# A gated feed-forward layer on one core: all 28 column tiles multiplied in pairs, first products of eight pairs run ahead, and two pairs' weights sent from a second queue

## The chip, the cores and the metric

The kernel runs on one core of one Trainium2 chip. The metric is the device time of one execution in microseconds (us); lower is better. Most executions of a kernel agree within a few tenths of a per cent; the profile is of one execution, and its span (first to last instruction) is some 2 us shorter than the device time. Each ratio is quoted with its 95% interval.

## The reference, cut to what matters

```python
B, S, D, F = 32, 32, 1024, 3584          # bfloat16 inputs
def reference(x, w_gate, w_up, w_down):
    return (gelu_tanh(x @ w_gate) * (x @ w_up)) @ w_down
```

There are 1024 rows of x. The kernel works transposed: 28 tiles of 128 columns of F, each over two halves of 512 rows (call them half 0 and half 1), with 8 contraction steps of 128 (k = 0 to 7) for gate and for up.

## The kernel before: the parts that matter

Two tiles (a "left" and a "right" one), two halves of the rows and two halves of k make a 2 x 2 by 2 x 2 block product. Done directly it takes 8 block products; the kernel does it with 7, in a scheme of sums and differences. Two of the seven multiply plain bf16 weights and plain x. The other five multiply *sums* of x (array `S`, made once) by *sums* of weights (array `T`, made for each pair), which are kept as fp32r (32-bit). One product is 8 matmuls of 128x128 by 128x512 (4 for gate, 4 for up).

A small scheduler sorts each engine's instructions (TensorE excepted, which keeps program order) by an `at` value and adds the semaphores. So `at` is an order and not a time: an engine that waits for one item holds up all behind it.

```python
# The opening: four tiles on half 0, directly, as the k blocks arrive ...
steps = [(m, j, k) for k in range(DK - KO) for j in range(2) for m in range(4)]
...
    op = mm(2 * m + j, first[:, j, k, tile(m)*P:(tile(m)+1)*P], xT[0][:, k, :], ...)
    if k == 3 and m < 2:                       # product 1 of pairs 0 and 1 is kept
        act(kept[m][:, j, :], bank(2 * m + j), COPY, 10.5)
    if (m, j) == (3, 1) and k == 3:            # second half of x: four DMA transposes
        for k0 in range(0, DK, 2): load_x(1, k0, k0 + 2, [op])
# ... then two of these tiles on half 1, directly (32 matmuls) ...
load_near(10)                                  # right-hand weights of pairs 0, 1   (1 MB, SyncE)
load_pairs(1, 0, 11, slice(0, 4))              # left-hand weights of pairs 2, 3    (1 MB, SyncE)
load_pairs(1, 0, 11, slice(4, 8))
load_pairs(1, 1, 12)                           # right-hand weights of pairs 2, 3   (1 MB, SyncE)
# ... then products 1 and 2 of pairs 2 and 3 run ahead (32 matmuls), while VectorE makes the sums
for p in (2, 3):
    ...
# ... then 13 pairs: EARLY = 4 of them have 5 products left (40 fp32r matmuls),
# the other 9 have all 7 (16 bf16 and 40 fp32r matmuls), then the down projection
for p in range(NP):
    short, last = p < EARLY, p == NP - 1
    ...
```

`load_x` is a DMA that transposes on its way in. Why products 1 and 2 run ahead: they need only weights and half 0 of x, so they give TensorE work while the sums are being made.

## Time and profile before

| | before |
|---|---|
| device time, median of 6 runs | 275.26 us |
| span of the profile | 272.7 us |
| TensorE (PE) busy | 268.1 us, 98% |
| VectorE / ScalarE busy | 69% / 46% |
| opening: 128 bf16 matmuls | 4.61 to 32.42 us |
| four early pairs: 160 fp32r matmuls | 32.42 to 69.15 us |
| a late pair | 12.56 us |

The page of the profile has the busy time of each engine, then the span cut in 40 slices with the busy share in tenths (PEclk is the granted clock of TensorE in tenths), then the chain of work that ended last.

```profile
PE 268.1 (98%) x1186; PEld 188.1 (69%) x1200; DVE 189.2 (69%) x221; ACT 125.7 (46%) x195; POOL 45.4 (17%) x27
...
PE   8999999999999999999999999999999999999995
...
PEclk9999999999999999999999999999999999999999
DMA  7999412954700090047005000995011000001112
...
PE 98%; issue 0%; DVE 0%
```

TensorE is never idle, at full clock, and the chain is TensorE alone: the time is the number of matmuls times their rate. The DMA row shows the one place where something else is near its limit: the first four slices (up to about 27 us) are full. (The share adds up the times of all DMA packets and divides by 16 engines; packets can overlap.)

The timeline of PE (columns: start, length, engine, line, operation, output and inputs, shapes, count):

```profile
4.61 28.16 PE L117 MATMUL ps<-arena 128*128 128x512 bf16 x126
32.42 36.66 PE L117 MATMUL ps<-S,T 128*128 128x512 f32 x160
69.15 1.67 PE L117 MATMUL ps<-arena 128*128 128x512 bf16 x7
```

The first line is the whole opening, in one piece. The second is the four early pairs: 36.73 us from start to start for 160 matmuls. (A few records of matmuls are missing, hence 126 for 128.) And the timeline of PE's weight loads in the middle of the opening; the bracket tells how long the weight loader was idle before, and what ended that:

```profile
25.56 0.55 PEld L117 LDWEIGHTS ps<-arena 128*128 128x128 bf16 x4 [0.33 <-DMA arena<-in_w_gate_dram]
26.47 0.55 PEld L117 LDWEIGHTS ps<-arena 128*128 128x128 bf16 x4 [0.36 <-DMA arena<-in_w_up_dram]
```

These are the weights of the second pair of tiles to run ahead. They come just as TensorE wants them, with nothing to spare.

### The profile page before, as it was taken

What the parts mean: (1) busy time and instruction counts of PE and PEld (TensorE: products, weight loads), DVE (VectorE), ACT (ScalarE), POOL (GpSimd) and SP (SyncE); (2) the same over time, 40 slices, a digit from 0 to 9 for tenths busy, and PEclk for the clock granted to TensorE, in tenths of its full rate; (3) what the DMA queues carried; (4) which work ended last, traced back from release to release, by engine and by line L of the source; (5) the groups of instructions that cost most, each with busy time, mean ns of one, the idle gap of its engine ahead of it and who ended that gap; (6) DMA issues with size and microseconds to landing.
All of it is one profiled execution on the core that took longest, in us unless ns stands there. A gap on an engine that the chain in (4) does not pass through costs nothing.

```text
span 272.7 us, 3266 instructions
## 1 busy us (share of the span) xinstructions
PE 268.1 (98%) x1186; PEld 188.1 (69%) x1200; DVE 189.2 (69%) x221; ACT 125.7 (46%) x195; POOL 45.4 (17%) x27
## 2 busy tenths in 40 slices
PE   8999999999999999999999999999999999999995
PEld 4444588888767686868676776664447888888884
DVE  1059978988583939374664739289962999999942
ACT  2344757566556474646455564521220112255561
POOL 1000032035326060524335160000000000000000
PEclk9999999999999999999999999999999999999999
DMA  7999412954700090047005000995011000001112
GB/s 184 270 207 300 117 39 60 281 202 124 186 0 0 21 286 2 0 129 179 1 4 154 0 2 0 302 350 159 0 38 38 2 0 0 1 2 58 38 58 77
DMA packets 44783, 26.42 MB, mean 97 GB/s; under 512 B 8416, under 2 KB 44768, under 8 KB 44768
## 3 DMA queue, kind: packets, MB, share of 16 engines
q1 hardware_dynamic: 42544, 24.25, 32.3%
q10 hardware_dynamic: 2224, 1.97, 2.8%
q8 instruction: 9, 0.15, 0.2%
q14 instruction: 6, 0.05, 0.1%
HBM read 22.28 MB, written 2.10 MB: 89 GB/s over the span
## 4 chain that ended last, share of the span: by engine, by line
PE 98%; issue 0%; DVE 0%
PE ps L117 98%; DVE arena L117 0%
## 5 line engine op out<-in xcount | busy, mean ns | idle before, releaser
L117 PE MATMUL ps<-S,T 128*128 128x512 f32 x520 | 122.0, 393 | 0.0
L117 PEld LDWEIGHTS ps<-S,T 128*128 128x128 f32 x520 | 97.7, 188 | 21.3
L117 ACT ACTIVATE tmp<-ps 128x512 f32<-128x512 f32 x64 | 38.1, 598 | 62.0 <-PE ps L117 62.0
L117 POOL TENSOR_TENSOR T<-arena 128x1024 fp32r<-128x1024 bf16 x21 | 44.7, 2149 | 117.1 <-PE ps L117 66.7
L117 PE MATMUL ps<-arena 128*128 128x512 bf16 x261 | 59.0, 379 | 0.8
L117 PE MATMUL ps<-T,S 128*128 128x512 f32 x224 | 51.3, 390 | 0.0
L117 ACT ACTIVATE ps<-ps 128x512 f32<-128x512 f32 x52 | 30.2, 583 | 42.0 <-PE ps L117 42.0
L117 DVE TENSOR_TENSOR hT<-tmp,ps 128x512 bf16<-128x512 f32 x56 | 37.2, 684 | 17.3 <-PE ps L117 14.9
L117 DVE TENSOR_TENSOR T<-arena,T 128x1024 fp32r<-128x1024 bf16 x40 | 48.4, 1217 | 0.1
L117 PEld LDWEIGHTS ps<-arena 128*128 128x128 bf16 x272 | 25.1, 98 | 33.4 <-issue 3.4
L117 PEld LDWEIGHTS ps<-T,S 128*128 128x128 f32 x224 | 42.1, 188 | 8.8
L117 DVE TENSOR_TENSOR tmp<-ps,tmp 128x512 f32<-128x512 f32 x26 | 18.0, 692 | 41.9 <-PE ps L117 41.9
L117 DVE TENSOR_TENSOR T<-arena 128x1024 fp32r<-128x1024 bf16 x19 | 22.7, 1218 | 7.4 <-PE ps L117 7.4
L117 PE MATMUL ps<-arena,hT 128*128 128x512 bf16 x109 | 24.0, 379 | 0.2
L117 DVE TENSOR_TENSOR ps<-ps,tmp 128x512 f32<-128x512 f32 x30 | 20.9, 695 | 2.8 <-PE ps L117 2.8
L117 PEld LDWEIGHTS ps<-arena,hT 128*128 128x128 bf16 x112 | 10.9, 98 | 13.2 <-issue 0.3
L117 ACT ACTIVATE tmp<-tmp 128x512 f32<-128x512 f32 x26 | 16.4, 632 | 4.2 <-DVE tmp L117 3.5
L117 DVE TENSOR_TENSOR S<-hT 128x1024 fp32r<-128x1024 bf16 x14 | 16.6, 1218 | 0.0
L117 ACT ACTIVATE T<-arena 128x1024 fp32r<-128x1024 bf16 x13 | 13.7, 1055 | 0.0
L117 PE MATMUL ps<-S 128*128 128x512 f32 x56 | 12.9, 389 | 0.0
L117 PEld LDWEIGHTS ps<-S 128*128 128x128 f32 x56 | 10.5, 188 | 2.2
L117 ACT ACTIVATE S<-arena 128x1024 fp32r<-128x1024 bf16 x9 | 9.4, 1057 | 4.3 <-PE ps L117 3.0
(25 smaller groups left out, 62.1 us busy)
## 6 DMA issues: line engine op xcount, KB each, us to landing
arena<-in_w_down_dram SPq DMA_DIRECT2D x4, 1792.0 KB, 10.5
arena<-in_w_gate_dram SPq DMA_DIRECT2D x11, 512.0 KB, 5.5
arena<-in_w_up_dram SPq DMA_DIRECT2D x11, 512.0 KB, 6.4
out_dram<-arena SPq DMA_DIRECT2D x12, 128.0 KB, 1.7
arena<-in_w_up_dram ACTq DMA_DIRECT2D x4, 128.0 KB, 4.5
arena<-in_w_gate_dram ACTq DMA_DIRECT2D x2, 256.0 KB, 5.0
arena<-in_w_up_dram ACTq DMA_DIRECT2D x2, 256.0 KB, 5.5
arena<-in_w_gate_dram SPq DMA_DIRECT2D x2, 256.0 KB, 6.3
```

The costliest lines, as they stand in the source:

```text
L117: ins = name(eng, *args, **kw) if callable(name) else getattr(eng, name)(*args, **kw)
```

## The change

Its intent is to do fewer matmuls. Before, tiles 0 and 1 stood outside the scheme, which costs them 8 products for 8. After, all 28 tiles form 14 pairs. The 32 direct matmuls on half 1 that filled the opening are gone, so something else must fill it while the sums are made: products 1 and 2 of four more pairs (now pairs 0 to 7 have them ahead). That brings a need for the weights of pairs 4 to 7 in the opening, and those of pairs 4 and 5 go out from ScalarE's DMA queue, past SyncE's queue, which is taken by the transposes of x. The diff, cut to its core (the new places in memory, and which engine copies what, are left out):

```diff
-        LEFT = [2, 3] + list(range(4, 14)) + [14]
-        RIGHT = [26, 27] + list(range(16, 26)) + [15]
-        NP, EARLY = len(LEFT), 4
+        NP, EARLY = 14, 8
...
-            if k == 3 and m < 2:
-                act(kept[m][:, j, :], bank(2 * m + j), COPY, 10.5)
+            if k == 3:
+                if m % 2 == 0:
+                    act(kept[m][:, j, :], bank(2 * m + j), COPY, 10.5)
+                else:
+                    pr.add("dve", "tensor_copy", kept[m][:, j, :], bank(2 * m + j), at=10.5)
...
-        steps = [(m, j, k) for m in range(2) for j in range(2) for k in range(KO)]   # tiles 0, 1 on half 1
-        ...
-        load_near(10)
-        load_pairs(1, 0, 11, slice(0, 4))
-        load_pairs(1, 0, 11, slice(4, 8))
-        load_pairs(1, 1, 12)
+        load_duo(2, 0, 12.5, "act", 2)     # left weights of pairs 4, 5, from ScalarE's queue
+        load_duo(0, 1, 10)                 # right weights of pairs 0, 1, SyncE's queue
+        load_duo(3, 0, 11, "sp", 2)        # left weights of pairs 6, 7, SyncE's queue, last
...
-        for p in (2, 3):
+        for p in range(4, EARLY):
...
-        sums_x(4, 22)
+        sums_x(4, 21.65)
         sums_w(0, 3, 28.6)
         t4 = sums_w(0, 4, 33.9)
+        load_duo(1, 1, 34)
...
-            if t % 2:
+            if t % 2 == 0:
                 pr.add("dve", "tensor_copy", late[:, 2, t, :], bank(PA[t]), at=at)
```

Below, "the megabyte" is the load of pairs 4 and 5 from ScalarE's queue (1.05 MB), and "the load for pair 6" is the last one in SyncE's queue.

More of the change, by code (lines that the diff above doesn't have):

```diff
@@ L161, in bass_standalone__geglu_ffn__sampling_kernel, with duo @@
         xT = [arena[:, a:a + 4096].rearrange("p (k n) -> p k n", n=512) for a in (16384, 0)]
-        raw_at = (20480, 8192)
-        raw = [arena[:, a:a + 8192].rearrange("p (s j k c) -> p s j k c", s=2, j=2, k=DK) for a in raw_at]
-        first = arena[:, raw_at[0]:raw_at[0] + 8192].rearrange("p (j k c) -> p j k c", j=2, k=DK)
-        near = arena[:, 4096:8192].rearrange("p (j k c) -> p j k c", j=2, k=DK)
+        first = arena[:, 20480:28672].rearrange("p (j k c) -> p j k c", j=2, k=DK)
+        def duo(a): return arena[:, a:a + 4096].rearrange("p (j k c) -> p j k c", j=2, k=DK)
         wd = [[arena[:, a:a + 7168].rearrange("p (k n) -> p k n", n=512) for a in row] for row in ((0, 7168), (14336, 21504))]
@@ L229, in bass_standalone__geglu_ffn__sampling_kernel, with piece @@
                 pr.add("dve", "tensor_copy", xT[0][:, k, i * 256:(i + 1) * 256], half)
-        LEFT = [2, 3] + list(range(4, 14)) + [14]
-        RIGHT = [26, 27] + list(range(16, 26)) + [15]
-        NP, EARLY = len(LEFT), 4
-        def left(p): return LEFT[p]
-        def right(p): return RIGHT[p]
-        kept = [hT[:, m:m + 2, :].rearrange("p t n -> p (t n)").bitcast(FP32).rearrange("p (j n) -> p j n", j=2)
-                for m in (10, 12, 22, 24)]
+        NP, EARLY = 14, 8
+        def piece(a): return a.rearrange("p t n -> p (t n)").bitcast(FP32).rearrange("p (j n) -> p j n", j=2)
+        kept = [piece(hT[:, m:m + 2, :]) for m in (8, 10, 12, 22, 24, 26, 20)] + [piece(o11[:, :, :])]
         SLOT = 0.9064
-        t0 = 33.0
+        t0 = 32.7
         T0 = []
@@ L257, in bass_standalone__geglu_ffn__sampling_kernel @@
             steps += [(m, j, k) for j in range(2) for k in range(DK - KO, DK)] + [(m, None, None)]
-        tile = lambda m: (m + 2) % 4
         for m, j, k in steps:
@@ L262, in bass_standalone__geglu_ffn__sampling_kernel @@
                 act(tmp[:, m, :], bank(2 * m), GELU, at)
-                tt(hT[:, tile(m), 0:512], tmp[:, m, :], bank(2 * m + 1), MUL, at)
+                tt(hT[:, m, 0:512], tmp[:, m, :], bank(2 * m + 1), MUL, at)
                 continue
-            op = mm(2 * m + j, first[:, j, k, tile(m) * P:(tile(m) + 1) * P], xT[0][:, k, :], k == 0, k in (3, DK - 1), add=k > 3)
-            if k == 3 and m < 2:
-                act(kept[m][:, j, :], bank(2 * m + j), COPY, 10.5)
+            op = mm(2 * m + j, first[:, j, k, m * P:(m + 1) * P], xT[0][:, k, :], k == 0, k in (3, DK - 1), add=k > 3)
+            if k == 3:
[3 more added lines that the diff above has]
+                    pr.add("dve", "tensor_copy", kept[m][:, j, :], bank(2 * m + j), at=10.5)
             if (m, j) == (3, 1):
@@ L274, in bass_standalone__geglu_ffn__sampling_kernel, with load_duo @@
                         load_x(1, k0, k0 + 2, [op])
-        steps = [(m, j, k) for m in range(2) for j in range(2) for k in range(KO)]
-        steps += [(m, j, k) for k in range(KO, DK - KO) for j in range(2) for m in range(2)]
-        for m in range(2):
-            steps += [(m, j, k) for j in range(2) for k in range(DK - KO, DK)] + [(m, None, None)]
-        for m, j, k in steps:
-            if j is None:
-                at = 25.0 + m * 0.87
-                act(tmp[:, m, :], bank(2 * m), GELU, at)
-                tt(hT[:, m, 512:1024], tmp[:, m, :], bank(2 * m + 1), MUL, at)
-                continue
-            mm(2 * m + j, first[:, j, k, m * P:(m + 1) * P], xT[1][:, k, :], k == 0, k == DK - 1)
-        def load_near(at):
-            for j in range(2):
-                dma("sp", near[:, j, :, :], w_r[j][:, :, right(0) * P:(right(1) + 1) * P], at, f"near{j}")
-        def load_pairs(gi, s, at, ks=slice(0, DK)):
-            for j in range(2):
-                m = (left, right)[s](2 * gi)
-                dma("sp", raw[gi % 2][:, s, j, ks, :], w_r[j][:, ks, m * P:(m + 2) * P], at, f"w{gi}_{j}{s}_{ks.start}")
-        load_near(10)
-        load_pairs(1, 0, 11, slice(0, 4))
-        load_pairs(1, 0, 11, slice(4, 8))
-        load_pairs(1, 1, 12)
+        PLACE = [(None, 4096), (None, 0), (8192, 4096), (12288, 0), (20480, 24576), (8192, 12288), (20480, 24576)]
+        def load_duo(g, s, at, eng="sp", parts=1):
+            m, n = 2 * g + 14 * s, DK // parts
+            for k in range(0, DK, n):
+                for j in range(2):
+                    dma(eng, duo(PLACE[g][s])[:, j, k:k + n, :], w_r[j][:, k:k + n, m * P:(m + 2) * P], at, f"w{g}{s}{j}{k}")
+        load_duo(2, 0, 12.5, "act", 2)
+        load_duo(0, 1, 10)
+        load_duo(3, 0, 11, "sp", 2)
         def load_wd(i, j, at):
@@ L307, in pair_w @@
         def pair_w(p, s, ks):
-            col = slice((p % 2) * P, (p % 2 + 1) * P)
-            if p < 2:
-                return first[:, :, ks, slice((p + 2) * P, (p + 3) * P)] if s == 0 else near[:, :, ks, col]
-            if p == NP - 1:
-                return raw[0][:, 0, :, ks, slice(s * P, (s + 1) * P)]
-            return raw[(p // 2) % 2][:, s, :, ks, col]
+            a = PLACE[p // 2][s]
+            if a is None:
+                return first[:, :, ks, p * P:(p + 1) * P]
+            return duo(a)[:, :, ks, (p % 2) * P:(p % 2 + 1) * P]
         def sx(s, k): return S[:, 4 * s + k:4 * s + k + 2, :]
@@ L329, in sums_x @@
                 else:
-                    act(sx(4, k), x1[:, k + 4:k + 6, :], COPY, at)
+                    act(sx(4, k), x1[:, k + 4:k + 6, :], COPY, at + 1.73 * k)
         def unit(p, u): return (5 * p + u) % 8
@@ L348, in stat @@
         def stat(p, j, k): return pair_w(p, 0, slice(k, k + 1))[:, j, 0, :]
-        for p in (2, 3):
-            at = 25.8 + (p - 2) * 3.46
-            g, u = 2 * p, 2 * p + 1
+        for p in range(4, EARLY):
+            at = 18.9 + (p - 4) * 3.46
+            g, u = 2 * p - 8, 2 * p - 7
             for b, j, k0 in ((g, 0, 0), (u, 1, 0), (g, 0, 4), (u, 1, 4)):
@@ L358, in bass_standalone__geglu_ffn__sampling_kernel @@
             act(tmp[:, p, :], bank(g), GELU, at + 2.7)
-            tt(hT[:, left(p), 0:512], tmp[:, p, :], bank(u), MUL, at + 3.6)
+            tt(hT[:, p, 0:512], tmp[:, p, :], bank(u), MUL, at + 3.6)
         sums_x(0, 21)
@@ L376, in bass_standalone__geglu_ffn__sampling_kernel @@
             A, E = ((0, 1), (2, 3)) if short or (p - EARLY) % 2 == 0 else ((2, 3), (0, 1))
-            if p % 2 == 0 and 2 <= p // 2 + 1 < (NP + 1) // 2:
-                load_pairs(p // 2 + 1, 0, t0)
-                if p < NP - 3:
-                    load_pairs(p // 2 + 1, 1, t0)
-            if p == 3:
+            for q, g, s in ((1, 2, 1), (3, 3, 1), (3, 4, 0), (3, 4, 1), (7, 5, 0), (7, 5, 1), (10, 6, 0), (10, 6, 1)):
+                if p == q:
+                    load_duo(g, s, t0)
+            if p == 7:
                 load_wd(0, 0, t0)
-            if last:
+            if p == 12:
                 load_wd(0, 1, t0)
-            ml, mr = left(p), right(p)
+            ml, mr = p, p + 14
             at = lambda s: t0 + s * SLOT
```

## The prediction

> **What bounds the kernel now.** TensorE. The page has PE 98% busy (268.1 of 272.7 us), the chain that ended last is PE for 98.3% of the span, the granted clock is 1.00; VectorE is at 69%, ScalarE at 46%. The time is the number of matmuls times their rate, plus what starves PE.
>
> **Rates, from the timeline of PE.** A late pair (16 bf16, 40 fp32r matmuls) repeats every 12.56 us (92.54 to 105.10). The 160 fp32r matmuls of the four early pairs take 36.7 us (32.42 to 69.1): one is 0.229 us, an early pair 9.17 us, a bf16 matmul (12.56 - 9.17)/16 = 0.212 us. The opening's 128 bf16 matmuls take 27.8 us (4.61 to 32.42), some 0.5 us more than 128 x 0.213.
>
> **By count.** The opening keeps 128 bf16 matmuls (64 + 32 + 32 before, 64 + 64 after). The pairs go from 4 early + 9 late (149.7 us) to 8 early + 6 late: 8 x 9.17 + 6 x 12.56 = 148.7 us. That is -1.0 us, all on PE, so all on the critical path: 48 bf16 matmuls go (-10.2 us), 40 fp32r come (+9.2). A pair costs 56 matmuls instead of 64, but 40 are the dearer kind. The last eviction moves from VectorE (692 ns) to ScalarE (597 ns): -0.1 us.
>
> **What it adds.** Four more pairs at the early rhythm: VectorE is 85% busy from 35 to 70 us and PE shows no gap there, so I expect none to 106 us. Four copies of first products move to VectorE at 10 to 13 us; four of 0.69 us must fit into some 2.8 us before PE wants the banks again: +0.1 us (0 to 0.3).
>
> **The risk: the opening's weights.** The windows show DMA saturated from 2 to 30 us. PE's weight loads wait for DMA at 25.56, 26.47, 27.36 and 28.27 us: weights come just in time. After the change 1 MB (pairs 4, 5) leaves ScalarE's queue at about 12.5 us, wanted at 18.4; pairs 6, 7, wanted at 25.2, stand last in SyncE's queue, where another load landed until 30.2. The Trainium skill ("Trainium Kernel Development and Optimization", Key Constraints) says that all queues share the same 16 DMA engines and interleave: a second queue makes no bandwidth. But from 15 to 20 us transposes alone move 185 GB/s, while mixed stretches (10 to 15 us) move 314, so part of the megabyte fills that hole. Before moves 1.7 MB from 12.5 to 20 us; with 1.05 MB more at 300 to 330 GB/s it ends at 20.8 to 21.6, so what stands behind is 0.8 to 1.6 us later, less what the filled hole hides: estimate +0.6 us on PE (0 to 2). The second half of x comes later too, but PE no longer reads it directly, and the sums have some 2 us of slack.
>
> **Sum.** 275.3 - 1.0 - 0.1 + 0.1 + 0.6 = 274.9 us, range 273.8 to 276.5. Faster by over 2%: 0.01; within: 0.97; slower: 0.02.
>
> **What would show it.** 320 fp32r matmuls in one run without a gap, about 73.4 us; late pairs still 12.56 us; weight loads waiting for DMA at 25 to 28 us; the first fp32r matmul at 32.4 to 34 us. If it stays at 32.4, the loads were free and the time is 274.2.
>
> **What would make it wrong.** ScalarE's load landing after 18.4 us; the second half of x so late that ScalarE's copies of it hold up the copies of first products; VectorE falling behind over eight early pairs; the down projection's weights late.

## The result, and the profile after

The changed kernel takes 279.77 us (median of 6 runs, 279.52 to 280.83) against 275.26 us. Ratios here are the mean time of one kernel's fast runs over that of the other's of the same rounds, so not quite the ratio of the medians quoted: 1.0169, 95% interval 1.0142 to 1.0195. That is within 2%, as forecast, but slower by 4.5 us where I had expected 0.4 us less, and outside my range.

The page after, the same rows:

```profile
PE 269.7 (97%) x1181; PEld 191.2 (69%) x1192; DVE 201.1 (72%) x235; ACT 130.6 (47%) x206; POOL 41.3 (15%) x25
...
PE   8999599999999999999999999999999999999995
...
PEclk9999799999999999999999999999999999999999
DMA  7999550410890504900190043096011000001112
...
PE 89%; DMA 5%; SPq 4%; issue 0%; ACT 0%
```

All the trouble is in the fifth slice (about 28 to 35 us): PE is at 5 tenths there, the granted clock at 7, and the chain now has 5% DMA and 4% of SyncE's sequencer (SPq) in it. The timeline of PE after:

```profile
14.72 13.20 PE L117 MATMUL ps<-arena 128*128 128x512 bf16 x59 [0.50 <-DMA arena<-in_w_up_dram]
30.86 8.55 PE L117 MATMUL ps<-arena 128*128 128x512 bf16 x32 [2.94 <-DMA arena<-in_w_gate_dram]
39.06 72.93 PE L117 MATMUL ps<-S,T 128*128 128x512 f32 x320
112.06 1.67 PE L117 MATMUL ps<-arena 128*128 128x512 bf16 x7
```

And PE's weight loads behind the gap:

```profile
30.86 0.13 PEld L117 LDWEIGHTS ps<-arena 128*128 128x128 bf16 x2 [3.43 <-DMA arena<-in_w_gate_dram]
31.27 0.15 PEld L117 LDWEIGHTS ps<-arena 128*128 128x128 bf16 x1 [0.28 <-issue]
31.69 0.15 PEld L117 LDWEIGHTS ps<-arena 128*128 128x128 bf16 x1 [0.28 <-issue]
```

From the first fp32r matmul on, everything went as planned: 39.06 to 275.12 us (the last eviction's start) is 236.1 us, where before took 32.42 to 269.88, 237.5 us. The change gains 1.4 us there. The opening (first bf16 matmul to first fp32r matmul) lost 6.6 us: 34.4 us against 27.8. In this profile the loss splits in three: the four direct tiles end 2.1 us later (the fourth GELU starts at 20.55 us; before, at 18.43); pair 6 begins at 30.86 us where before the same matmul began at 25.56, another 3.2 us, of which 2.94 us is the gap before it; and the last 32 matmuls take 8.20 us instead of 6.86, because eight or so of them start 0.42 us apart, twice the usual, while the granted clock is at half.

### The profile page after: what moved, and what is told of

Read it like the earlier page. It is cut to its first block, busy times and chain, and to the rows that moved or that the text cites. A ratio compares the mean times of both kernels' runs of the same rounds, so it can differ in the third digit from the quotient of the medians.

```text
span 277.9 us, 3273 instructions
## 1 busy us (share of the span) xinstructions
PE 269.7 (97%) x1181; PEld 191.2 (69%) x1192; DVE 201.1 (72%) x235; ACT 130.6 (47%) x206; POOL 41.3 (15%) x25
## 4 chain that ended last, share of the span: by engine, by line
PE 89%; DMA 5%; SPq 4%; issue 0%; ACT 0%
PE ps L117 89%; SPq L117 4%; DMA arena<-in_x_dram 3%; DMA arena<-in_w_gate_dram 3%; ACT arena L117 0%
## 5 line engine op out<-in xcount | busy, mean ns | idle before, releaser
L117 PE MATMUL ps<-S,T 128*128 128x512 f32 x560 | 130.0, 392 | 0.0
L117 PEld LDWEIGHTS ps<-S,T 128*128 128x128 f32 x560 | 105.1, 188 | 22.6
L117 POOL TENSOR_TENSOR T<-arena 128x1024 fp32r<-128x1024 bf16 x19 | 40.6, 2150 | 126.4 <-PE ps L117 79.2
L117 PE MATMUL ps<-arena 128*128 128x512 bf16 x216 | 51.5, 391 | 4.4 <-DMA arena<-in_w_gate_dram 2.9
L117 DVE TENSOR_TENSOR T<-arena,T 128x1024 fp32r<-128x1024 bf16 x42 | 50.9, 1219 | 0.1
L117 ACT ACTIVATE ps<-ps 128x512 f32<-128x512 f32 x48 | 27.9, 583 | 39.3 <-PE ps L117 39.3
L117 PEld LDWEIGHTS ps<-arena 128*128 128x128 bf16 x224 | 21.0, 100 | 33.9 <-issue 6.7
L117 DVE TENSOR_TENSOR T<-arena 128x1024 fp32r<-128x1024 bf16 x23 | 27.5, 1220 | 8.8 <-PE ps L117 7.4
L117 DVE TENSOR_TENSOR ps<-ps,tmp 128x512 f32<-128x512 f32 x32 | 22.3, 696 | 3.0 <-PE ps L117 3.0
L117 ACT ACTIVATE hT<-ps 128x512 f32<-128x512 f32 x10 | 5.6, 599 | 12.5 <-PE ps L117 12.5
```

Of the source, the lines that this page charges most:

```text
L117: ins = name(eng, *args, **kw) if callable(name) else getattr(eng, name)(*args, **kw)
```

## The experiments

Three reasons had to be told apart: the transfers land late (and why); the gap costs more than its length, through the clock; and the first 2.1 us, most of which come before the change has sent anything new, are chance. All runs gave correct results unless it is said that they are wrong on purpose.

### A second profile of before

No edit.

> The kernel before, unchanged, for a second profile of it. Theory A (the slower first 14 us of the changed kernel's profile are chance or come with its program as a whole): if chance, the first-half tiles end (the fourth GELU out of the opening) at 18.4 us here within about 0.5 us, or wander by up to 2 us. Theory B (the change itself makes them slower): always 18.4 us here, always about 20.5 us in every run that keeps the change's opening. First fp32r matmul at 32.4 us, time about 275.3 us.

One run, 274.7 us, span 272.5 us. The fourth GELU starts at 18.28 us, the first fp32r matmul at 32.21 us. So before's opening repeats.

### Pairs 6 and 7 read weights that lie ready (wrong)

```diff
-                    mm(b, stat(p, j, k), x0[:, k, :], ...)
+                    mm(b, stat(p if p < 6 else p - 6, j, k), x0[:, k, :], ...)
```

> The changed kernel, but the early products of pairs 6 and 7 read the weights of pairs 0 and 1, which lie ready (wrong result on purpose); the transfers all stay. Theory 1 (PE starves for the last load in SyncE's queue, and the clock falls after the gap): the 2.9 us gap before pair 6 and the slow matmuls at half the granted clock (1.35 us) both go, the first fp32r matmul starts near 35 us instead of 39.1, time near 275.5 to 276.5 us. Rival (the sums of x and of the first pair's weights are late as well, and the gap only hides that): the first fp32r matmul or the ones after it wait for VectorE, and the time stays above 278 us.

275.05 us (4 runs), ratio to before 0.9987 (0.9969 to 1.0005). All transfers stay, only TensorE's wait for the last one is gone, and with it 4.7 us of the changed kernel's median (taken in another set of runs). The opening is in one piece again, and the clock record stays at full. The rival is right in a smaller part: the fp32r matmuls now wait, through ScalarE, for VectorE, whose first weight sum started at 28.55 us, just after the right-hand weights of pairs 0 and 1 had landed (28.47 us; 25.15 us in the run without the megabyte, below). In the timeline of PE:

```profile
32.32 3.12 PE L117 MATMUL ps<-S,T 128*128 128x512 f32 x12
36.20 70.74 PE L117 MATMUL ps<-S,T 128*128 128x512 f32 x308 [0.76 <-ACT ps L117]
```

The first 12 take 3.88 us where 12 at 0.229 us would be 2.75: 1.1 us lost. In this run the fourth GELU is at 18.33 us, so the slow first 20 us of the changed kernel's profile are not tied to its opening's instructions, which up to there are the same here.

### The order in SyncE's queue turned round

```diff
-        load_duo(0, 1, 10)
-        load_duo(3, 0, 11, "sp", 2)
+        load_duo(3, 0, 10, "sp", 2)
+        load_duo(0, 1, 11)
```

> Only the order in SyncE's queue is turned round: the weights of pairs 6 and 7 go before the right-hand weights of pairs 0 and 1. Theory 1: the first pieces for pair 6 land about 3.5 us earlier (near 27.3 us instead of 30.8), the gap of 2.9 us shrinks to under 0.5 us, the granted clock does not fall; the first pair's weight sums now wait for the other load (to about 31 us) and may cost PE up to 1 us. Time about 276.5 us (275.5 to 277.5). Rival (bandwidth as a whole is short and any order loses the same): time stays within 1 us of 279.8.

277.99 us (4 runs), ratio 1.0093 (1.0065 to 1.012). The first piece for pair 6 landed at 26.05 us, the gap before pair 6 went, and the matmuls kept their full rate (this trace has no clock record; they start 0.216 us apart). But another gap opened further on. The timeline of PE, and under it that of ScalarE:

```profile
33.53 1.90 PE L117 MATMUL ps<-arena 128*128 128x512 bf16 x8 [2.00 <-ACT o L117]
35.08 3.10 PE L117 MATMUL ps<-S,T 128*128 128x512 f32 x12
39.58 70.74 PE L117 MATMUL ps<-S,T 128*128 128x512 f32 x308 [1.40 <-ACT ps L117]
```

```profile
31.93 1.06 ACT L117 ACTIVATE T<-arena 128x1024 fp32r<-128x1024 bf16 x1 [2.35 <-DMA arena<-in_w_up_dram]
32.89 1.07 ACT L117 ACTIVATE o<-ps 128x512 f32<-128x512 f32 x2
```

ScalarE's queue holds, in this order, a copy of the first pair's right-hand weights (`T<-arena`) and the copies of pair 7's first products (`o<-ps`), which TensorE waits for. The first now waits 2.35 us for the load that was put last, and holds up the second. My expectation had looked only at VectorE. Both it and the rival missed the time.

### The same, with VectorE's order changed too

```diff
-        sums_x(2, 28)
+        sums_x(2, 23.5)
-        sums_x(3, 30.3)
+        sums_x(3, 24)
```

> As the run before it, and the third and fourth sums of x go ahead of the first weight sums in VectorE's order, so that VectorE works while that load is still under way. Theory 1: no PE gap is left over 0.5 us in the opening but what the first 14 us show, the first fp32r matmul near 34.7 us, time about 275.5 us (274.0 to 276.5). If the weight sums of the first pair are still late, PE waits for VectorE at 35 to 40 us and the time is no better than the run before it.

275.87 us (4 runs), ratio 1.0031 (0.9986 to 1.0076). One of the four took 278.27 us: its mean granted clock was 0.994, that of the others 1.000, so one execution in four lost the clock here too. VectorE's part of the wait is gone: the 320 fp32r matmuls run in one piece from 35.06 us. ScalarE's gap of 1.84 us is still there. The expectation of no gap over 0.5 us did not hold.

### And ScalarE's copy moved behind

```diff
-        sums_w(0, 3, 28.6)
+        sums_w(0, 3, 32.1)
```

> The reordered kernel, and ScalarE's copy of the first pair's weights (which stood ahead of the copies of pair 7's first products and waited 2.3 us for its load) goes behind them. Theory: ScalarE's queue order alone made the 1.84 us gap, so it goes, the first fp32r matmul starts near 33.2 us, time near 274.0 us (273.5 to 274.6), faster than before by 0.5%. Rival (pair 7's products or the sums behind them wait for something else just as late): the time stays at 275.5 us or more.

275.19 us (4 runs) beside 275.13 for before, ratio 0.9987 (0.996 to 1.0014). The gap of 1.84 us went, as its theory said (first fp32r matmul at 33.07 us), but only 0.7 us of the median came with it, and that between two sets of runs, in the second of which before was 0.4 us faster as well. The time missed its theory's 274.0 us. The first 12 fp32r matmuls now took 3.99 us instead of 2.75, with a wait for VectorE's weight sum:

```profile
34.77 2.06 PE L117 MATMUL ps<-S,T 128*128 128x512 f32 x8 [0.43 <-DVE T L117]
```

So the time that I took from one wait went in part into the next. This is what a full opening looks like: PE, DMA and VectorE all have little slack there.

### The changed kernel again

No edit.

> The changed kernel again, for a second profile and its time beside the others. Theory A (the 2.1 us that its first profile lost before 20.5 us is chance of that profile or chip): the fourth GELU starts near 18.4 to 18.9 us, the gap before pair 6 is still 2 to 3 us, time 277.5 to 278.5 us. Theory B (it belongs to the change): the fourth GELU again near 20.5 us, time 279.5 to 280.5 us.

279.45 us (4 runs), ratio 1.0138 (1.0109 to 1.0167). The fourth GELU is at 19.37 us, so about half of the 2.1 us did not come again; but the gap before pair 6 grew to 3.85 us, and pair 6 began at 30.60 us, against 30.86. The time hardly changed. What decides, as I read it, is when the load for pair 6 lands; lateness ahead of it only shortens the gap. Neither theory's numbers held.

### The gap filled with idle work

```diff
+            if p == 6:
+                for n in range(10):
+                    mm(g, one[:, 0:P], one[:, :], True, True)    # constants, overwritten at once
```

> The changed kernel with ten matmuls of constants ahead of pair 6, in a bank that is about to be overwritten; they take 2.1 us in the gap, where PE waits for the load anyhow. Theory 1 (a gap of nearly 3 us makes the granted clock fall, and the next 8 matmuls run at half speed): the granted clock stays 1.00, the matmuls after the gap come every 0.21 us, 1.3 us come back, time 278.4 us against 279.8 (or 1.3 us under the run of the changed kernel beside it). Rival (the slow matmuls are paced by the landing of the load, not the clock): nothing comes back, time as the changed kernel beside it, or up to 0.5 us more.

276.93 us (4 runs), ratio 1.0051 (1.0025 to 1.0077): 2.5 us less than the changed kernel beside it, by doing *more* matmuls. In the timeline of PE:

```profile
26.12 2.35 PE L117 MATMUL ps<-const-bfloat16-1.0 128*128 128x512 bf16 x10
29.24 7.16 PE L117 MATMUL ps<-arena 128*128 128x512 bf16 x32 [0.77 <-DMA arena<-in_w_gate_dram]
36.04 72.93 PE L117 MATMUL ps<-S,T 128*128 128x512 f32 x320
```

The windows view tells of the clock (for each stretch: its length, busy time and count for each engine, then the granted clock, the DMA share, GB/s); first the changed kernel, then this one:

```profile
31.00:36.00 5.00, 5.00 (x17) 1.81 (x16) 5.00 (x6) 2.14 (x4) 0.00 (x0) 0.73 0.06 15
```

```profile
31.00:36.00 5.00, 5.00 (x24) 2.04 (x24) 5.00 (x6) 3.77 (x6) 0.00 (x0) 1.00 0.16 45
```

In the same 5 us the changed kernel has 17 matmuls, "100% busy", at a clock of 0.73; this one 24 at full clock. The 32 matmuls behind the gap take 6.80 us here and 8.37 us in the second profile of the changed kernel: 1.6 us from the clock. But 2.5 us came back. The rest of it was open at this point.

### The filled gap and the changed kernel once more

No new edit; five rounds each, beside each other.

> The changed kernel with ten matmuls of constants in the gap, again. It came out 2.5 us under the changed kernel, where its theory allowed 1.3 to 1.6 us. If the clock is all, the difference from the changed kernel beside it is 1.3 to 1.7 us over five rounds, and the load for pair 6 lands equally late in both (30.5 us); if 2.5 us come back again, something besides the clock is earlier in it, and the landing of that load (29.2 us in its first profile) is earlier again.

> The changed kernel beside the run with the filled gap, for the same question. Granted clock half for 3.4 us after the gap before pair 6; time 279.0 to 280.0 us if the first two results hold, 278.3 us if the opening of its profiles was unlucky.

With the gap filled 277.03 us (6 runs, ratio 1.0074, 1.0055 to 1.0092); unfilled 278.19 us (6 runs, ratio 1.0114, 1.0086 to 1.0141). The six runs of the unfilled kernel fall in two groups by their mean granted clock:

```
changed kernel:  279.34 (0.993)  279.11 (0.994)  278.94 (0.994)   mean 279.13
                 277.18 (1.000)  277.05 (1.000)  277.45 (1.000)   mean 277.23
filled gap:      277.37  276.23  278.08  277.11  276.73  276.94   mean 277.08, clock 1.000 in all
```

So executions in which the clock drops are 1.9 us longer than others of the same kernel; 1.6 us of that is seen in the matmuls behind the gap. With the gap filled, none of 10 executions lost the clock. In this set a run of the changed kernel that escapes the drop equals the filled one, so the means of the two kernels are only 1.1 us apart, less than the expectation's 1.3 to 1.7. In the set before, the changed kernel had lost the clock in 3 of 4 runs (279.29 to 279.74 us; the fourth, at full clock, 278.39). Three times 1.9 us over four runs is 1.4 us of the 2.5. The rest fits chance in the first 12.5 us, in which the filled kernel's profile had moved DMA at 222 GB/s and the other at 199: its load landed 1.4 us earlier (29.19 against 30.55 us). In this pair of runs (205 and 201 GB/s) it landed at 29.71 and 30.13 us. All six runs of the changed kernel's first set had lost the clock, three of them about twice as much (mean clock 0.987 against 0.993 and 0.994); no profile shows why.

### Without the megabyte (wrong)

```diff
-                    mm(b, stat(p, j, k), x0[:, k, :], ...)
+                    mm(b, stat(p if p > 5 else p - 4, j, k), x0[:, k, :], ...)
...
-        load_duo(2, 0, 12.5, "act", 2)
...
         load_duo(1, 1, 34)
+        load_duo(2, 0, 34.1)
```

> The changed kernel without ScalarE's load in the opening: pairs 4 and 5 read the weights of pairs 0 and 1 for their early products (wrong result on purpose), and their own load goes out on SyncE's queue after 34 us. Theory 1 (that megabyte pushes x's second half and everything behind it back): the last of x's second half lands near 21.2 us instead of 22.9 to 24.1, the first piece for pair 6 near 25.5 us instead of 30.8, no gap before pair 6, time 273.8 us (273.3 to 274.6). Rival (a second queue costs nothing, the order within SyncE's queue is at fault): the gap before pair 6 stays over 2 us.

273.74 us (4 runs), ratio to before 0.9934 (0.9905 to 0.9962). This is the gain of the change without its cost: everything is there except one megabyte in the opening (which also leaves it with less to load than before). The opening is in one piece, and the fp32r run starts at 32.94 us:

```profile
4.79 28.50 PE L117 MATMUL ps<-arena 128*128 128x512 bf16 x128
32.94 12.41 PE L117 MATMUL ps<-S,T 128*128 128x512 f32 x53
```

The landings that the traces record, in us:

```
                                     before   no megabyte   changed kernel (three profiles)
last piece of x's second half         21.17      19.82        24.11   23.89   23.46
first quarter of the load for pair 6  25.52      26.06        30.82   30.55   30.13
                                     (before: the load in the same place of the queue)
```

The megabyte makes the load for pair 6 land 4.1 to 4.8 us later. Of this, 3.8 to 4.4 us had passed when SyncE issued it (19.04 us without the megabyte, 22.82 to 23.43 with it): SyncE came late to it behind the transposes. Where the time went is told by the windows view from 12.5 to 26 us and from 17 to 22 us. Before, then without the megabyte, then the changed kernel (second profile):

```profile
12.50:26.00 13.50, 13.45 (x63) 5.98 (x63) 8.63 (x10) 5.60 (x9) 0.00 (x0) 1.00 1.07 261
17.00:22.00 5.00, 5.00 (x25) 2.29 (x24) 4.10 (x6) 3.25 (x5) 0.00 (x0) 1.00 0.95 232
```

```profile
12.50:26.00 13.50, 13.50 (x64) 5.70 (x62) 9.28 (x12) 7.42 (x14) 0.00 (x0) 1.00 1.10 261
17.00:22.00 5.00, 5.00 (x24) 2.09 (x23) 4.46 (x6) 2.99 (x6) 0.00 (x0) 1.00 0.96 218
```

```profile
12.50:26.00 13.50, 13.50 (x64) 5.74 (x63) 7.26 (x11) 7.41 (x13) 0.00 (x0) 1.00 1.14 251
17.00:22.00 5.00, 5.00 (x24) 2.18 (x23) 2.75 (x4) 3.24 (x6) 0.00 (x0) 1.00 1.25 226
```

Read the last two numbers. In this profile the second queue raised the DMA share, from 0.95 to 1.25 in the inner window, and moved no more bytes: 226 GB/s against 232 and 218, and over the whole stretch 251 against 261 and 261. But what one window shows depends on where it is cut, so here are all three profiles of the changed kernel, in GB/s:

```
                before   no megabyte   changed kernel (three profiles)
12.5 to 26 us     261        261          267   251   260
17 to 22 us       232        218          259   226   230
12.5 to 20 us     227        236          279   266   270
20 to 26 us       303        292          252   232   248
```

Two lines of this as the windows view has them, without the megabyte and with it (third profile):

```profile
12.50:20.00 7.50, 7.50 (x36) 3.39 (x35) 3.65 (x6) 2.94 (x6) 0.00 (x0) 1.00 1.08 236
12.50:20.00 7.50, 7.45 (x35) 3.38 (x35) 3.65 (x6) 2.90 (x6) 0.00 (x0) 1.00 1.21 270
```

Up to 20 us the second queue did move more: some 0.2 to 0.3 MB over the 7.5 us against the run without the megabyte, about a quarter of the megabyte. From 20 to 26 us, where x's transposes now still ran, the rate fell by 40 to 70 GB/s and took it back. Over the whole stretch the megabyte took the place of another megabyte. At 260 GB/s 1.05 MB is 4.0 us, close to the 4.1 to 4.8 us measured.

### Half of the megabyte (wrong)

```diff
-                    mm(b, stat(p, j, k), x0[:, k, :], ...)
+                    mm(b, stat(p if p > 5 or k < 4 else p - 4, j, k), x0[:, k, :], ...)
...
-        load_duo(2, 0, 12.5, "act", 2)
+        load_duo(2, 0, 12.5, "act", 2, (0, 4))      # k 0 to 3 only
...
+        load_duo(2, 0, 34.1, "sp", 2, (4, 8))
```

> The changed kernel, but ScalarE's queue loads only the first half (k 0 to 3) of the weights of pairs 4 and 5 in the opening, half a megabyte; the other half goes out on SyncE's queue after 34 us and the early products read weights that lie ready in its place (wrong result on purpose). Theory 1 (every byte is added to a DMA system that has no hole): about half the delay, the last piece of x's second half near 22 us (19.8 without the load, 23.9 with all of it), the first piece for pair 6 near 28.3 us (26.1 and 30.6), time about 275.5 to 276.5 us. Rival (my prediction's hole: what runs beside the transposes is mostly free, and only the rest costs): the first half costs little, the first piece for pair 6 at 26.8 us or sooner, time under 274.7 us.

274.62 us (4 runs), ratio 0.9984 (0.9971 to 0.9997). The first quarter for pair 6 landed at 27.01 us, x's last piece at 22.08 us, the gap is 1.00 us. The total moved from 12.5 to 26 us is the same again (257 GB/s), as Theory 1 has it; but the delay of the load for pair 6 is not in proportion: 0.95 us for the first half megabyte, 3.1 to 3.8 us for the second. By its numbers this is nearer to the rival. So some of a smaller load is hidden, and the second half is paid in full and more. x's second half, for which TensorE does not wait, was 2.3 us later than without the load; that it gave way in place of the load for pair 6 is my reading and was not tested. From 12.5 to 20 us this run moved 268 GB/s, as much as with the whole megabyte, so it seems that half of it used up the little room that there is. Why the second half costs more than the 2.0 us that half a megabyte takes at 260 GB/s stays open.

### A version from all of it

The reordered run with ScalarE's copy moved, with the right-hand weights of pairs 0 and 1 in two parts, so that the first weight sum needs only half of them, and with VectorE's order chosen by what lands when:

```diff
-        load_duo(0, 1, 10)
-        load_duo(3, 0, 11, "sp", 2)
+        load_duo(3, 0, 10, "sp", 2)
+        load_duo(0, 1, 11, "sp", 2)
-        sums_w(0, 0, 24.5)
-        sums_w(0, 1, 27)
-        sums_x(2, 28)
-        sums_w(0, 2, 29)
-        sums_x(3, 30.3)
+        sums_w(0, 0, 29.5)
+        sums_w(0, 1, 29.6)
+        sums_x(2, 26.5)
+        sums_w(0, 2, 29.7)
+        sums_x(3, 33)
-        sums_w(0, 3, 28.6)
+        sums_w(0, 3, 32.1)
```

> The run with the reordered loads and ScalarE's copy moved, and two things more: the right-hand weights of pairs 0 and 1 come in two parts along k, so that the first weight sum needs only half of them, and VectorE's order is sums 1, 2, 3 of x, then the weight sums, then sum 4 of x. Theory: the 1.2 us that PE lost there between its first and twelfth fp32r matmul (it waited for VectorE's weight sum) go; the first fp32r matmul near 33 us and 320 of them in a row in 73 us, time 274.2 us (273.6 to 274.8), faster than before by 0.4%. Rival (VectorE is simply too full in the opening): the wait only moves and the time stays at 275.2 us.

274.61 us (6 runs, 274.21 to 274.91) beside 274.95 us for before, ratio 0.9987 (0.9975 to 0.9998). It is correct, 3.6 us under the changed kernel of the same set of runs, and just under before: 0.1%, at the edge of what the interval can tell. The run with ScalarE's copy moved had the same ratio, 0.9987, with a wider interval, so no gain in time is shown for the two further edits. In the profile the wait was made smaller, not removed:

```profile
32.82 1.28 PE L117 MATMUL ps<-S,T 128*128 128x512 f32 x4
34.52 71.89 PE L117 MATMUL ps<-S,T 128*128 128x512 f32 x316 [0.42 <-ACT ps L117]
```

Four matmuls take 1.70 us instead of 0.92. The kernel without the megabyte, at 273.74 us, shows that about 1 us more lies in the opening, if a megabyte less had to be loaded there.

## Why the prediction was wrong, point by point

- **What bounds the kernel: right.** TensorE, by count times rate.
- **The gain by count: right in kind, a little too small.** I expected -1.0 us and -0.1 us for the last eviction. Measured, from the first fp32r matmul to the start of the last eviction, -1.4 us; the eviction itself shrank from 0.69 to 0.60 us. The run of 320 took 73.0 us (39.06 to 112.06; I had said 73.4) without a gap, and a late pair still takes as long (12.55 us, 135.46 to 148.01 in the chain of waits). Without the megabyte the whole gain is there (ratio 0.9934).
- **VectorE over eight early pairs: right.** No gap in the 320. The four copies moved to VectorE cost nothing that shows: from k = 4 on, the direct tiles take 6.9 us in the run without the megabyte as in before.
- **The failed step: "part of the megabyte fills that hole", and so "what stands behind is 0.8 to 1.6 us later, ... estimate +0.6 us on PE".** I took the 185 GB/s from 15 to 20 us for spare bandwidth that would be filled up to 300 to 330. With the second queue the stretch from 12.5 to 20 us moved 266 to 279 GB/s, not 300 to 330: some 0.2 to 0.3 MB of the megabyte found room. And this was no gain in the end, because the transposes themselves were drawn out (x's last piece landed 3.6 to 4.3 us later than without the megabyte), so that the next 6 us moved less, and from 12.5 to 26 us the sum was what it had been. The load for pair 6 came 4.1 to 4.8 us later, and the gap was 2.9 to 3.9 us instead of 0.6. A sign of it stood in the profile of before: the DMA share from 15 to 20 us was already 0.91. The figure of 300 to 330 GB/s for a mixed stretch came from a window in which large rows of weights (the four tiles' 1 KB rows) made up most of the bytes (1.00 of 1.57 MB). The prediction also compared with the wrong load: it took the one that stood last before (30.2 us; the trace has 30.00 and 31.50), but the load in the place that pair 6's took landed from 25.52 us on, just as TensorE wanted it, so there was no slack to lose.
- **A cost that I had not listed: the clock.** In all three profiles of the changed kernel a gap of 2.9 to 3.9 us went with 3.41 us at half clock. Executions that it strikes are 1.9 us longer, and it is one reason why a stall of some 3 us goes with an opening that is 6.6 us longer. I had read PEclk 1.00 before and taken it for given.
- **The list of what could go wrong was partly right.** ScalarE's queue order did hold up first products, but only once the load order was turned round. The second half of x did come 2 to 3 us later; no run separates what that alone costs. What did cost time, once the gap was gone (1.1 us in the run with pairs 6 and 7 on ready weights), was VectorE's first weight sum behind a load that had come late. ScalarE's load came in time for pair 4.
- **Chance, it seems, and not the change:** the fourth GELU started between 18.3 and 20.6 us in the twelve profiles that share the direct tiles' part of that opening. Full clock is first granted between 3.5 and 6.5 us by the traces' clock records, and x's first pieces land at different times; which of them makes how much of it was not tested.

What stays open: why bytes hardly add beside transposes, whether SyncE came late because the engines were shared or because something in the issuing itself was (no run tells the two apart), and the uneven cost of the two half megabytes.

The Trainium skill ("Trainium Kernel Development and Optimization", Key Constraints) says that issuing from several engines "only saves the sequencer's issue time". I quoted it and then did not follow it to its end; over the stretch from 12.5 to 26 us the traces agree with it (251 to 267 GB/s with the second queue, 261 without), though from 12.5 to 20 us alone the second queue moved 30 to 43 GB/s more than the run without the megabyte. The skill also says ("DMA: Bandwidth & Descriptors", Queues, rings and completion order) that a DMA engine takes turns between queues packet by packet. The trace agrees in direction: beside ScalarE's load SyncE issued x's last transposes at 13.72, 15.96 and 19.34 us (third profile of the changed kernel), without it at 13.75, 15.10 and 16.45 us; no run here shows the turns themselves.

## What to carry to other kernels

Before adding a transfer to a busy stretch, read the DMA share beside the GB/s: here a stretch of slow transposes at 0.91 to 1.03 had room for a quarter of a megabyte and not for a whole one, and the second queue mostly changed who came first. Compare the bytes over several windows before calling a hole filled or not. Even where the sum of bytes in a stretch stays the same, as here, it matters what is wanted first. Move a needed load forward by moving another one back, and then look at every in-order engine whose queue has something that waits for the one moved back. Where TensorE must wait some 3 us, a few matmuls of constants into a bank about to be overwritten can keep its clock: here none of 10 executions lost it, and to lose it cost 1.9 us.

## What the Trainium skill lacked or had wrong

- "TensorE: Matmul & The Clock Gate" (Part 1, and HAM oscillation) describes windows of 3.413 us and full or half rate, and the clock records here agree: half rate for 3.41 us, and matmuls 0.42 us apart in it. But its rule there, no idle gaps over about 3.4 us (its table of goals has about 3), is too generous: a gap of 2.94 us lost the clock. Half rate began at 30.30 us; if the window before it ended there, it ran from 26.89 us, and TensorE was idle in it from 27.92 us, some 2.4 of its 3.4 us. In the reordered run with VectorE's order changed, a gap of 1.84 us left the clock record at full, though one unprofiled execution of that kernel in four lost the clock (0.994). In the third set of the changed kernel it was lost in 3 executions of 6; how long the gap was in the other three is not known.
- The same page says in one place that the moment when full clock is first granted varies by about 0.5 us either way. Across the eleven traces here that have a clock record it lay between 3.48 and 6.5 us after the first instruction, for kernels that start alike (the first matmul is at 0.77 us in all).
- "DMA: Bandwidth & Descriptors" (Latency and other measured facts) gives 261 GB/s for transposing DMAs with a non-contiguous middle dimension, and more for contiguous ones. With transposes alone in flight this kernel moved 210 GB/s (15 to 17 us of before). The page says nothing of the bandwidth of plain loads beside a transpose; here 1.05 MB from a second queue left the sum from 12.5 to 26 us at 251 to 267 GB/s, against 261 without it.
